# Attention with the order of each engine given in the source, scores and maxima in single PSUM banks, and q and k laid out turned

## The chip, the cores and the metric

The kernel runs on one core of a Trainium2 chip. Its engines are PE (matrix products; PEld is its weight load), DVE (vector), ACT (scalar functions), POOL (GpSimd) and SP, which here only issues DMA transfers. PE writes to PSUM, eight banks of 512 fp32 words in each of 128 partitions; DVE and ACT read PSUM, POOL does not. The metric is the device time of one launch in microseconds, as the median of several runs.

## The reference

Block-sparse attention over 4 batches of 8 heads, 768 positions and 64 features, followed by a feed-forward part:

```python
scores = scale * np.matmul(q, k.transpose(0, 1, 3, 2))
mask = np.abs(blk_i - blk_j) <= window                    # blocks of 32, window 1
mask = mask | (blk_i == 0) | (blk_j == 0) | (blk_i == n_blocks - 1) | (blk_j == n_blocks - 1)
...                                                       # and three sampled blocks per row of blocks
scores = np.where(mask, scores, -1000000000.0)
scores = scores - np.max(scores, axis=-1, keepdims=True)
attn = np.exp(scores)
attn = attn / (np.sum(attn, axis=-1, keepdims=True) + 1e-09)
x = np.matmul(attn, v)                                    # heads joined: 3072 tokens x 512
h = x @ w_in                                              # 512 x 2048
out = (h - np.tanh(h)) @ w_out                            # 2048 x 512
```

All of it is in fp32. The kernel reaches that precision by splitting each factor into a high and a low part and adding up products of the parts.

## The kernel before, in words

The 32 heads are worked on in 16 pairs. A pair's q and k come from DRAM with the positions in partitions (`load`). `prep_qk` (line 192) transposes each of them on PE in six steps (line 198), copies the result to an fp32r tile on ACT (the high part, line 200) and subtracts that from it on DVE (the low part, line 201). `dist` (line 204) then spreads the parts by twelve DMA transfers of 64 partitions over four operands, `sA` to `sD`, in one of three slots of SBUF, where the rows 64 to 87 hold the mask as 24 rows of blocks (`fill`) and row 88 of `sB` the negative row maximum. One matmul with 88 or 89 rows so adds the mask, and with row 88 the maximum, to a product of the high parts.

Per head there are six key tiles of 128 keys, each against all 768 queries. Each passes these steps:

- `smax` (line 248): the products of the high parts with 128 queries against all keys in 512 + 256 columns, in a PSUM tile of two banks, and a maximum over them on DVE (line 259). After six of these `smax_fin` (line 261) turns the maxima on PE, scales them on DVE (line 266) and sends them to row 88 of `sB` by a DMA that SP issues (line 267). These maxima run about ten tiles ahead of the scores.
- `qk_exp` (line 276): the scores, turned (keys in partitions), in 512 + 256 columns of two passes each (lines 283 and 284), in a PSUM tile of two banks, and one exponential of 768 columns on ACT to `pe` (line 287).
- `split` (line 290): `ph`, an fp16 copy of `pe` (on ACT, line 297, or for two tiles of twelve on DVE, line 295), and `pl`, the fp16 rest (line 299), on POOL, or for one tile of twelve on DVE.
- `accum` (line 303): 18 matmuls of 64 or 65 columns that add the tile's products of `ph` and `pl` with the parts of v. After six tiles `norm` (line 325) divides by the sum of the row, and `spill` writes the pair's result to DRAM.

`prep_v` (line 217) scales and splits v for each pair, with the low part on DVE (line 241). Six of the feed-forward part's weight tiles are loaded and converted from their 8-byte words during attention (`load_pre` and `convert_pre`); each conversion is three DVE instructions (`convert`, lines 436, 439 and 442).

PSUM holds three tiles of two banks (scores, maxima and the transposes share them) and two of one bank (the `accum` sums, the turned maxima, the sum for v).

The order of the work comes from a list of events, each with a time in units of one key tile (`at`, the constants in lines 55 to 62), sorted by time. The framework then places the instructions by a timeline of its own and may reorder them within an engine; three kinds of added dependences hold it back: a chain through the PE work from head 5 on (`in_order`), the first loads (`after`), and the value products in pairs (line 317). Whatever it chooses, each engine's sequence is fixed before the launch, and each engine runs its sequence in that order. Every DMA is issued by SP.

`FFN` is the feed-forward part. Its first two steps are placed at the end of attention, and the rest (`rest`, line 611) follows when attention's PSUM is free.

Of the kernel before, what the change touches and what calls it, by code (L numbers as in the profile page):

```python
# [106 lines left out]
def attention(ctx, tc, q, k, v, samp, w_in, w_out, blocks, xscr, ident, ps, slots, wt, f2, ffn):  # L107
    nc = tc.nc
    big, one = ps
# [6 lines left out]
    loads = {}


    chain = []

    def in_order(h, first, last):
        if h < CH0:
            return
        if chain:
            tc.add_manual_dep(
                first.ins, chain[-1].ins.name, mybir.DependencyInfo(mybir.DependencyClass.NoSync, mybir.DependencyReason.DATA), reason="order"
            )
        chain.append(last)  # L130


    urgent = [[], [], []]

    def after(n, d):
        for f in urgent[n]:
            tc.add_manual_dep(
                d.ins, f.ins.name, mybir.DependencyInfo(mybir.DependencyClass.NoSync, mybir.DependencyReason.DATA), reason="first pair"
            )

    def load(pr, which="kqv", first=None):
        r = loads.setdefault(pr, [])
        for nm, src in ((n, x) for n, x in (("k", k), ("q", q), ("v", v)) if n in which):
            t = p2.tile([P, S], F32, tag="raw" + nm, name=f"raw{nm}{pr}", bufs=2)
            d = nc.sync.dma_start(out=t, in_=src[pr])
            r.append(t)
            if pr <= 3 and first is not None:
                after(first, d)

    load(0, "kq")  # L150
# [534 lines left out]
```

## Time and profile before

| | us |
|---|---|
| median of three runs | 985.01 |
| lowest and highest of them | 983.36 and 985.48 |
| span of the profiled execution, first to last instruction | 983.2 |

The profile gives no time of the profiled execution other than its span; the median of the runs stands 1.8 us above it. Over the span PE is busy 94%, DVE 75%, ACT 64% and POOL 47% of the time, as an average over attention and the feed-forward part. In the rows below a group reads: line, engine, operation, output<-inputs, shapes, number of instructions | busy time in us, mean length of one in ns | idle time of the engine before them, and what ended it. A timeline row reads: start, length, engine, line, operation, number, and in brackets the engine's idle time before it. In the windows each engine has its busy time in us and, in brackets, its number of instructions; PEclk is the granted clock of PE, and the DMA share that of 16 DMA engines.

### The profile page before, as it was taken

Reading aid. Unit: us, or ns where it says so; the run is one execution under the profiler, and the core shown is the slowest. Engines: PE = TensorE matmul, PEld = TensorE weight load, DVE = VectorE, ACT = ScalarE, POOL = GpSimd, SP = SyncE. Lnnn points to the kernel's source line nnn. Section 1 sums busy time; section 2 is a strip of 40 time slices with the busy share of each in tenths; the row PEclk is TensorE's granted clock in tenths of the full one; section 3 lists DMA queues with packets and bytes.
Section 4 is the critical chain, followed back from the end, with each engine's and each line's share of the span. In section 5 each row is a group of like instructions: output and inputs, shape, how many; then the busy total and the mean of one; then the engine's idle time right before and its main releaser. Section 6 shows DMA issues by size and latency. Waiting matters only on the chain.

```text
span 983.2 us, 18548 instructions
## 1 busy us (share of the span) xinstructions
PE 922.6 (94%) x7264; PEld 771.1 (78%) x7264; DVE 733.4 (75%) x1119; ACT 629.7 (64%) x943; POOL 458.3 (47%) x308
## 2 busy tenths in 40 slices
PE   5788999999999999888999999999999999999997
PEld 3577788887888878767788888888888888888885
DVE  4589888887887878859999876765676666566664
ACT  1476888888888878656666665555555465555553
POOL 1365877777777777754445422222222222222221
PEclk9698999999999999898999999999999999999999
DMA  8796777676676667114451220210020000001001
GB/s 231 185 274 190 195 175 175 162 174 162 168 173 162 162 161 189 45 48 157 148 168 50 65 76 11 97 33 12 1 75 1 1 33 11 1 1 44 1 1 43
DMA packets 56263, 99.78 MB, mean 101 GB/s; under 512 B 6008, under 2 KB 26680, under 8 KB 56176
## 3 DMA queue, kind: packets, MB, share of 16 engines
q1 hardware_dynamic: 56176, 98.60, 37.0%
q8 instruction: 57, 0.93, 0.4%
q14 instruction: 30, 0.25, 0.1%
HBM read 44.64 MB, written 15.20 MB: 61 GB/s over the span
## 4 chain that ended last, share of the span: by engine, by line
PE 77%; ACT 6%; DMA 5%; DVE 5%; issue 3%; SPq 1%; POOL 1%; ACTq 0%; POOLq 0%; DVEq 0%
PE pf L537 25%; PE pf L569 8%; PE pf L570 8%; PE pf L571 8%; PE st L283 6%; PE st L284 5%; PE sm L255 5%; ACT pe L287 3%; PE av L313 2%; PE av L321 2%; PE av L322 2%; DMA slot<-lok 2%; DMA slot<-nm 2%; DVE mc L259 1%; PE pf L451 1%
## 5 line engine op out<-in xcount | busy, mean ns | idle before, releaser
L299 POOL TENSOR_TENSOR pl<-pe,ph 128x768 f16<-128x768 f32 x173 | 290.0, 1692 | 130.5 <-ACT ph L297 67.5
L560 POOL TENSOR_TENSOR gl<-t,gh 128x512 fp32r<-128x512 f32 x96 | 124.0, 1292 | 358.4 <-ACT gh L559 307.0
L259 DVE TENSOR_REDUCE mc<-sm 128x1 f32<-128x768 f32 x192 | 181.0, 951 | 53.1 <-PE sm L255 49.2
L287 ACT ACTIVATE pe<-st 128x768 f32<-128x768 f32 x192 | 154.1, 805 | 78.4 <-PE st L284 68.5
L283 PE MATMUL st<-slot 128*128 128x512 f32 (+1 forms) x384 | 146.4, 382 | 17.1 <-ACT pe L287 13.4
L552 DVE TENSOR_TENSOR t<-t,pf 128x512 f32<-128x512 f32 x94 | 64.5, 686 | 123.3 <-ACT t L546 123.2
L559 ACT ACTIVATE gh<-t 128x512 fp32r<-128x512 f32 x96 | 60.6, 632 | 120.2 <-DVE t L556 120.2
L297 ACT ACTIVATE ph<-pe 128x768 f16<-128x768 f32 x154 | 130.0, 844 | 4.7
L284 PE MATMUL st<-slot 89*128 89x512 f32 (+1 forms) x384 | 126.1, 349 | 1.0 <-DMA slot<-nm 1.0
L313 PE MATMUL av<-vhl,ph 128*128 128x65 f16 x1152 | 120.7, 195 | 0.0
L322 PE MATMUL av<-vhl,pl 128*128 128x65 f16 x1152 | 119.6, 194 | 0.9 <-POOL pl L299 0.9
L255 PE MATMUL sm<-slot 88*128 88x512 f32 (+1 forms) x384 | 111.1, 376 | 9.6 <-DMA slot<-hiq 7.0
L321 PE MATMUL av<-vhl,ph 128*128 128x64 f16 x1152 | 119.7, 196 | 0.0
L313 PEld LDWEIGHTS <-ph 128*128 128x128 f16 x1152 | 106.6, 97 | 13.6 <-issue 12.9
L322 PEld LDWEIGHTS <-pl 128*128 128x128 f16 x1152 | 107.9, 100 | 3.0 <-issue 1.5
L321 PEld LDWEIGHTS <-ph 128*128 128x128 f16 x1152 | 107.9, 98 | 0.7 <-issue 0.5
L544 ACT ACTIVATE u<-pf 128x512 f32<-128x512 f32 x94 | 56.2, 598 | 80.5 <-PE pf L537 80.2
L283 PEld LDWEIGHTS st<-slot 128*128 128x128 f32 x384 | 74.9, 195 | 35.1 <-ACT pe L287 18.5
L284 PEld LDWEIGHTS st<-slot 89*128 89x128 f32 x384 | 75.5, 197 | 11.2 <-DMA slot<-nm 2.2
L255 PEld LDWEIGHTS sm<-slot 88*128 88x128 f32 x384 | 62.6, 202 | 17.0 <-DMA slot<-mk 6.3
L570 PE MATMUL pf<-wx,gh 128*128 128x512 f32 x192 | 74.7, 389 | 0.0
L569 PE MATMUL pf<-wx,gh 128*128 128x512 f32 x192 | 74.7, 389 | 0.0
(123 smaller groups left out, 1962.8 us busy)
## 6 DMA issues: line engine op xcount, KB each, us to landing
slot<-hik SPq DMA_DIRECT2D x64, 192.0 KB
slot<-hiq SPq DMA_DIRECT2D x64, 192.0 KB
stage<-w_in SPq DMA_DIRECT2D x13, 512.0 KB
stage<-w_out SPq DMA_DIRECT2D x13, 512.0 KB
rawk<-k SPq DMA_DIRECT2D x16, 384.0 KB
rawq<-q SPq DMA_DIRECT2D x16, 384.0 KB
slot<-lok SPq DMA_DIRECT2D x32, 192.0 KB
slot<-loq SPq DMA_DIRECT2D x32, 192.0 KB
```

What stands on the lines that cost most here:

```text
L255: nc.tensor.matmul(pm[:, c], lhsT=sB[s][0:88, j, t * P : (t + 1) * P], rhs=sA[s][0:88, j, c], start=True, stop=True)
L259: maxed.append(nc.vector.tensor_reduce(out=mcs[h][:, t : t + 1], in_=pm[:, 0:S], op=ALU.max, axis=AX.X))
L283: ms.append(nc.tensor.matmul(st[:, c], lhsT=sC[s][:, j, kc], rhs=sD[s][:, j, c], start=True, stop=False))
L284: ms.append(nc.tensor.matmul(st[:, c], lhsT=sA[s][0:89, j, kc], rhs=sB[s][0:89, j, c], start=False, stop=True))
L287: nc.scalar.activation(out=pe, in_=st[:, 0:S], func=AF.Exp, scale=0.125)
L299: d = eng.tensor_tensor(out=pl, in0=pe, in1=ph, op=ALU.subtract)
L313: m = nc.tensor.matmul(o[:, t, :], lhsT=ph[:, c], rhs=vv[:, 0:65], start=(kt == 0 and t == 0), stop=False, skip_group_check=True)
L321: nc.tensor.matmul(o[:, t, 0:64], lhsT=ph[:, c], rhs=vv[:, 65:129], start=False, stop=False, skip_group_check=True)
L322: m = nc.tensor.matmul(o[:, t, :], lhsT=pl[:, c], rhs=vv[:, 0:65], start=False, stop=last, skip_group_check=True)
L537: nc.tensor.matmul(h, lhsT=w[:, cc], rhs=x[:, c, :], start=(k == 0), stop=(k == 3 * NCT - 1))
L569: nc.tensor.matmul(o, lhsT=gh[:, c], rhs=wo[0][ft], start=(ft == f0), stop=False)
L570: nc.tensor.matmul(o, lhsT=gh[:, c], rhs=wo[1][ft], start=False, stop=False)
```

## The change

- **Order.** In attention, and in the feed-forward steps placed within it, every call to an engine goes through a wrapper (`InOrder`) that tells the framework to keep the instruction at its place in the program order of its engine. The sorted list of events so is the order of each engine, SP's issues included; the three kinds of added dependences are gone. The steps are cut finer, so that the list can interleave them.
- **q and k.** They are stored in DRAM turned, with two heads' features in the 128 partitions and k and q side by side, as one array `kq`, loaded by one DMA per pair. The raw fp32 words are spread as the high parts. For the low parts DVE clears the low 12 bits (`mask_words`, two instructions of 768 words) and the rest is found by a subtraction (`low_words`, k's on DVE, q's on POOL). The PE transposes, the ACT copies and the subtractions from PSUM are gone. The number and size of the spreading DMAs is as before.
- **PSUM.** Six single banks are used in turn for scores, maxima and the small turned tiles, and two hold the `accum` sums of even and odd heads. Two key tiles (1536 columns) take three banks: 512, 256 + 256, and 512 columns. Each bank has an exponential of 512 columns on ACT and a maximum on DVE; the six tiles' two partial maxima are joined by one more small DVE instruction a head.
- **Casts.** `pe`, `ph` and `pl` are tiles for two key tiles (1536 columns). ACT copies in two halves; for one of six such tiles DVE copies it at once; `pl` is always one POOL instruction of 1536 columns.
- **Places.** The maxima run 8 units (key tiles) ahead of the scores at the start and 12 later. The turned maxima of a head go out 3.25 units ahead of its scores in the steady stage. The first pair's q and k and the first two heads' maxima are issued on ACT's DMA queue. The weight conversions are spread, with an instruction every two units, three of each 24. The feed-forward part's first staged weights are loaded near the end of attention.

```diff
-W0, DW = 40, 24.7
+W0, DW = 42.9, 24
-PB = 8
+PB = 4
+NPE = 3
-TQK, TV, TSM, LSP, LAV = -15.1, -5.6, -9.95, 2.1, 4.2
-PL_DVE = (11,)
-PL_DVE_END = (2, 5, 8, 11)
-PH_DVE = (4, 10)
+LEAD = 12
+LAV = 5.35
+PH_DVE = (3,)
+RAMP, NRAMP = 4, 24
+LATE = {2: (14, 10, 6), 3: (8, 4, 3), 4: (5, 3, 2), 5: (2, 1, 1), 6: (1, 0.5, 0.5)}
...
+            def call(*args, **kw):
+                r = f(*args, **kw)
+                self.tc.keep_in_program_order(r)
+                return r
...
-        big = actx.enter_context(tc.tile_pool(name="ps_big", bufs=3, space=PSUM))
-        one = actx.enter_context(tc.tile_pool(name="ps_one", bufs=2, space=PSUM))
+        psum = actx.enter_context(tc.tile_pool(name="psum", bufs=1, space=PSUM))
+        banks = [psum.tile([P, 512], F32, name=f"ps{i}") for i in range(8)]
+        turn = iter(range(10**6))
+        ps = lambda: banks[next(turn) % 6], banks[6:]
...
+    def load_x(pr):
+        raws[pr] = p2.tile([P, 2 * S], F32, tag="rawx", name=f"rawx{pr}", bufs=2)
+        if pr:
+            nc.sync.dma_start(out=raws[pr], in_=kq[pr])
+        else:
+            for x in range(2):
+                nc.scalar.dma_start(out=raws[pr][:, half(pr, x)], in_=kq[pr][:, half(pr, x)])
...
-        for t in range(T):
-            nc.tensor.transpose(pt[:, t * P : (t + 1) * P], raw[:, t * P : (t + 1) * P], ident)
-        ptv = pt[:, 0:S]
-        nc.scalar.activation(out=hi, in_=ptv, func=AF.Copy)
-        nc.vector.tensor_tensor(out=lo, in0=ptv, in1=hi.bitcast(F32), op=ALU.subtract)
...
+    def mask_words(pr, x):
+        if x == 0:
+            los[pr] = p2.tile([P, 2 * S], F32, tag="lo", name=f"lo{pr}", bufs=2)
+        c = half(pr, x)
+        nc.vector.tensor_scalar(
+            out=los[pr].bitcast(I32)[:, c], in0=raws[pr].bitcast(I32)[:, c], scalar1=-4096, scalar2=None, op0=ALU.bitwise_and
+        )
+
+    def low_words(pr, x, eng):
+        c = half(pr, x)
+        eng.tensor_tensor(out=los[pr][:, c], in0=raws[pr][:, c], in1=los[pr][:, c], op=ALU.subtract)
...
+    PIECES = (((0, 0, 512),), ((0, 512, S), (1, 0, 256)), ((1, 256, S),))
...
+    def smax(n, x):
...
+        b = sms[n, x] = bank()
+        for e, c, o in pieces(x):
+            t = 2 * m + e
+            nc.tensor.matmul(b[:, o], lhsT=sB[s][0:88, j, t * P : (t + 1) * P], rhs=sA[s][0:88, j, c], start=True, stop=True, skip_group_check=True)
+
+    def most(n, x):
...
+        if x == 1:
+            nc.vector.tensor_reduce(out=mcs[h][:, o : o + 2], in_=b.rearrange("p (e c) -> p e c", e=2), op=ALU.max, axis=AX.X)
+        else:
+            nc.vector.tensor_reduce(out=mcs[h][:, o : o + 1], in_=b, op=ALU.max, axis=AX.X)
...
+    def most_send(h):
...
+        (nc.sync if h > 1 else nc.scalar).dma_start(
...
+    def scores(n, x):
...
+        for e, c, o in pieces(x):
+            kc = slice((2 * m + e) * P, (2 * m + e + 1) * P)
+            nc.tensor.matmul(b[:, o], lhsT=sC[s][:, j, kc], rhs=sD[s][:, j, c], start=True, stop=False, skip_group_check=True)
+            nc.tensor.matmul(b[:, o], lhsT=sA[s][0:89, j, kc], rhs=sB[s][0:89, j, c], start=False, stop=True, skip_group_check=True)
+
+    def exps(n, x):
+        if x == 0:
+            pes[n] = p2.tile([P, 2 * S], F32, tag="pe", name=f"pe{n}", bufs=NPE)
+        nc.scalar.activation(out=pes[n][:, 512 * x : 512 * (x + 1)], in_=sts.pop((n, x)), func=AF.Exp, scale=0.125)
+
+    def high(n, e):
...
+        if n % 6 not in PH_DVE:
+            c = half(None, e)
+            nc.scalar.activation(out=phs[n][:, c], in_=pes[n][:, c], func=AF.Copy)
+        elif e:
+            nc.vector.tensor_copy(out=phs[n], in_=pes[n])
+
+    def low(n):
+        pls[n] = p2.tile([P, 2 * S], F16, tag="pl", name=f"pl{n}", bufs=PB)
+        nc.gpsimd.tensor_tensor(out=pls[n], in0=pes.pop(n), in1=phs[n], op=ALU.subtract)
...
+    def smt(n):
+        return 2 * n - LEAD + RAMP * max(0, 1 - n / NRAMP)
+
+    for h in range(2 * NPAIR):
+        t0 = smt(3 * h + 2)
+        late = 0 if h < 4 else 2
+        at(t0 + 1.6, most_join, h)
+        at(t0 + 2.5 + late, most_turn, h)
+        at(t0 + 2.75 + late, most_send, h)
+        at(6 * h + 10.3, norm, h)
+    for n in range(6 * NPAIR):
+        for x in range(3):
+            at(2 * n + 0.45 * x, scores, n, x)
+            at(smt(n) + 0.45 * x + 0.25, smax, n, x)
+            at(smt(n) + 0.45 * x + 0.6, most, n, x)
+            at(2 * n + 0.45 * x + 0.4, exps, n, x)
+        at(2 * n + 1, high, n, 0)
+        at(2 * n + 1.6, high, n, 1)
+        at(2 * n + 1.7, low, n)
+        at(2 * n + LAV, accum, n)
...
     for x in range(2 * NPRE):
         at(W0 + DW * x, load_pre, "io"[x % 2], x // 2)
-        at(W0 + DW * x + 4, convert_pre, "io"[x % 2], x // 2)
+        for k in range(3):
+            at(W0 + DW * x + 6 + 2 * k, convert_pre, "io"[x % 2], x // 2, k)
...
-        "q": pairs(inputs["q"], 0, 2, 3, 1, 4),
-        "k": pairs(inputs["k"], 0, 2, 3, 1, 4),
+        "kq": np.concatenate([pairs(inputs[n], 0, 1, 4, 3, 2) for n in "kq"], axis=2),
```

More of the change, by code (lines that the diff above doesn't have):

```diff
@@ L116, in attention, with load_v, load_masks, ones @@
     sA, sB, sC, sD = ([slots[i][:, x] for i in range(NSLOT)] for x in range(4))
[L118 to L150, printed above, removed]
+    raws, rvs, los, ams, sbs = {}, {}, {}, {}, {}
+    R = slice(64, 88)
+    st_sb = acst.tile([P, 2 * NB + S], F32, name="st_sb")
+    mk = p2.tile([P, S], F32, tag="pe", name="mk", bufs=NPE)
+    onehot = st_sb[:, 2 * NB : 2 * NB + S]
+    def load_x(pr):
[5 more added lines that the diff above has]
+                nc.scalar.dma_start(out=raws[pr][:, half(pr, x)], in_=kq[pr][:, half(pr, x)])
+    def load_v(pr):
+        rvs[pr] = p2.tile([P, S], F32, tag="rawv", name=f"rawv{pr}", bufs=2)
+        nc.sync.dma_start(out=rvs[pr], in_=v[pr])
+    sp_i = acst.tile([P, 6], I32, name="sp_i")
+    def load_masks():
+        nc.sync.dma_start(out=sp_i[R, :], in_=samp)
+        nc.sync.dma_start(out=st_sb[R, :], in_=blocks)
+    def ones(i):
+        nc.gpsimd.memset(sA[i].bitcast(F32)[64:89], 1.0)
     def setup():
@@ L217, in prep_v, with fill @@
[L217 to L232 removed]
+    def fill(i, dst, src):
+        nc.sync.dma_start(out=dst[i].bitcast(F32)[R], in_=src[R, :].unsqueeze(1).to_broadcast([NB, 2, S]))
@@ L234, in prep_v, with v_turn, v_scale @@
+    def v_turn(pr):
+        am, ams[pr] = ams[pr], bank()[:, 0:P]
+        nc.tensor.matmul(ams[pr], lhsT=am.to_broadcast([P, P]), rhs=ident, start=True, stop=True)
+    def v_scale(pr):
+        sb = sbs[pr] = p2.tile([P, 1], F32, tag="sb", name=f"sb{pr}", bufs=4)
+        nc.vector.tensor_reduce(out=sb, in_=ams.pop(pr), op=ALU.max, axis=AX.X)
         sbi = sb.bitcast(I32)
@@ L249, in smax @@
+    mcs, sms = {}, {}
+    def smax(n, x):
+        h, m = divmod(n, T // 2)
         pr, j = divmod(h, 2)
         s = pr % NSLOT
[L251 to L259 removed]
@@ L303, in accum @@
[L303 to L323 removed]
+        b = sts[n, x] = bank()
@@ L354, in attention @@
-    at(TQK + 0.3, fill, 0, sA, mask, 0)
-    at(TQK + 0.9, load, 1, "kq", 0)
-    at(TQK + 1.7, load, 0, "v", 1)
-    for i in range(1, NSLOT):
-        for dst, src in ((sB, onehot), (sA, mask)):
-            at(TQK + TF * i, fill, i, dst, src, 1)
+    at(-50, load_masks)
+    for i in range(NSLOT):
+        at(-48, ones, i)
+    at(-47, setup)
+    at(-46, fill, 0, sB, onehot)
+    at(-26.5, fill, 0, sA, mk)
+    for i, t in ((1, -4.5), (2, 6)):
+        at(t, fill, i, sB, onehot)
+        at(t + 0.5, fill, i, sA, mk)
@@ new lines, in attention @@
+        when = (s - 29.2, s - 25.2, s - 23.2) if pr > 1 else (-1, 0.7, 2.8) if pr else (-28, -28, -28)
+        at(when[0], mask_words, pr, 0)
+        at(when[1], mask_words, pr, 1)
+        at(when[2], low_words, pr, 0, nc.vector)
+        at(when[2], low_words, pr, 1, nc.gpsimd)
+        for x, (j, what) in enumerate(ORDER):
+            at(t0 + late[2] - 21 + x if pr > 1 else x - 3 if pr else EARLY[x], dist, pr, j, what)
+        s = t0 + (10.5, 4)[pr] if pr < 2 else t0
+        at(s - 9.3, v_most, pr)
```

308 lines of the change are left out of this document (119 added, 189 removed).

## The prediction

> **What bounds the kernel now.** First the windows of all engines, cut at the first exponential, where the pace settles, at the last exponential, and where the feed-forward part is at pace; then the same windows for the exponentials alone (L287).
>
> ```profile
> span 983.2 us, 18548 instructions
> ...
> core 0: us, PE busy (x) PEld busy (x) DVE busy (x) ACT busy (x) POOL busy (x), PEclk, DMA share, GB/s
> 33.40:105.20 71.80, 63.56 (x704) 52.89 (x703) 60.54 (x89) 49.57 (x62) 47.39 (x27) 0.88 0.80 226
> 105.20:428.30 323.10, 304.47 (x4060) 262.60 (x4059) 264.14 (x402) 265.29 (x339) 245.51 (x150) 0.99 0.62 155
> 428.30:446.00 17.70, 9.65 (x97) 7.69 (x96) 9.85 (x18) 5.99 (x11) 4.81 (x3) 0.82 0.35 111
> 446.00:983.20 537.20, 529.79 (x2360) 436.64 (x2360) 383.24 (x584) 304.34 (x529) 155.93 (x121) 0.99 0.14 45
> ...
> 33.40:105.20 71.80, 24.16 (x30) 0.88 0.80 226
> 105.20:428.30 323.10, 129.91 (x162) 0.99 0.62 155
> ```
>
> The last 537 us are the feed-forward part, with PE full; the change leaves them alone. Attention has two stages. Steady: 162 key tiles in 323.1 us, 1.994 each, 23.9 us per pair of heads (12 tiles), over 13.5 pairs. Start: the first exponential at 33.4, then 30 tiles in 71.8 us where the steady pace needs 59.8. In the steady stage DVE and ACT are busy 82% and POOL 76%; PE's 94% is partly the modelled ends. So next, PE's starts (start, length, line):
>
> ```profile
> 252.15 0.82 PE L198 MATMUL ptk<-ident,rawk 128*128 128x128 f32 x6
> 252.80 0.27 PE L264 MATMUL pmt<-ident,mc 128*6 128x128 f32 x1
> ...
> 259.24 0.20 PE L313 MATMUL av<-vhl,ph 128*128 128x65 f16 x1
> ...
> 260.35 0.48 PE L283 MATMUL st<-slot 128*128 128x512 f32 x1
> ...
> 261.16 0.51 PE L255 MATMUL sm<-slot 88*128 88x512 f32 x2
> 261.50 0.40 PE L283 MATMUL st<-slot 128*128 128x512 f32 x1
> ```
>
> Two tiles' value products take 260.35 - 259.24 = 1.11 us, one tile's scores and maxima products 261.50 - 260.35 = 1.15. Two tiles: 3.41; a pair of heads 20.5, and 1.3 more for twelve transposes (0.65 per six): 21.8 of 23.9. PE leads, but nothing is full; the rest is lost in turns between engines.
>
> **The change, part by part, for one pair of heads.** The prices, by groups of instructions (the L299 and L295 rows of DVE are of the steady stage alone), then three single instructions:
>
> ```profile
> L259 DVE TENSOR_REDUCE mc<-sm 128x1 f32<-128x768 f32 x192 | 181.0, 951 | 53.1 <-PE sm L255 49.2 <-PE av L322 1.8
> L552 DVE TENSOR_TENSOR t<-t,pf 128x512 f32<-128x512 f32 x94 | 64.5, 686 | 123.3 <-ACT t L546 123.2
> L299 DVE TENSOR_TENSOR pl<-pe,ph 128x768 f16<-128x768 f32 x16 | 24.8, 1551 | 2.6 <-ACT ph L297 1.7
> L295 DVE CAST ph<-pe 128x768 f16<-128x768 f32 x32 | 22.2, 693 | 6.0 <-ACT pe L287 6.0
> L201 DVE TENSOR_TENSOR lok<-ptk,hik 128x768 fp32r<-128x768 f32 x16 | 15.2, 947 | 0.0
> L287 ACT ACTIVATE pe<-st 128x768 f32<-128x768 f32 x192 | 154.1, 805 | 78.4 <-PE st L284 68.5 <-POOL pl L299 8.1 <-POOL slot L498 0.7
> L546 ACT ACTIVATE t<-pf 128x512 f32<-128x512 f32 x94 | 55.8, 593 | 0.2 <-POOL gl L560 0.2
> L200 ACT ACTIVATE hik<-ptk 128x768 fp32r<-128x768 f32 x16 | 12.8, 797 | 18.7 <-DVE mc L259 13.1 <-PE ptk L198 5.6
> L560 POOL TENSOR_TENSOR gl<-t,gh 128x512 fp32r<-128x512 f32 x96 | 124.0, 1292 | 358.4 <-ACT gh L559 307.0 <-issue 29.8 <-PE pf L537 21.0
> ...
> 109.79 3.25 POOL L299 TENSOR_TENSOR pl<-pe,ph 128x768 f16<-128x768 f32 x2
> 46.01 0.55 DVE L295 CAST ph<-pe 128x768 f16<-128x768 f32 x1
> 63.97 0.94 DVE L299 TENSOR_TENSOR pl<-pe,ph 128x768 f16<-128x768 f32 x1
> ```
>
> *PE.* The transposes go: -1.3. Scores and maxima keep their columns and their count of matmuls (512 + 256 + 256 + 512 over two tiles instead of twice 512 + 256). PE: 20.5.
>
> *ACT.* Three 512-wide exponentials for two tiles instead of two 768-wide: 3 x 0.593 - 2 x 0.805 = +0.17, +1.0 per pair; the two copies L200 go, -1.6. Casts stay 768 wide. Net -0.6 from 265.3/13.5 = 19.7. ACT is no bound.
>
> *DVE.* Maxima 3 x 0.686 (the nearest 512-wide row that reads PSUM) - 2 x 0.951 = +0.16, +0.9 per pair; two small joins, no row, between nothing and 0.3 each, taken at 0.3 together. L201 goes, -1.9; in come two mask operations of 768 words (nearest row the 0.55 cast, upper end 0.95) and one subtraction from SBUF (0.94). The DVE share of `pl` goes (-0.94); two casts of 0.55 become one of twice the width (0.55 to 1.1, taken 0.95). The weight conversions, now all in the start, are spread out, 18 instructions over the 16 pairs: 18 x 0.6 / 16 = +0.65 (nearest row L552). Today's 264.1/13.5 = 19.6 holds 0.9 of waiting (1.55 for a 0.94 subtraction, 2 x 0.14 in the casts), so 18.7 becomes about 19.6 without waits.
>
> *POOL.* All `pl` now run here, as six instructions of 1536 elements, and q's subtraction of 768 fp32 words (1.65 as the 768 row, or 768/512 x 1.292 = 1.94; taken 1.75). Two 768s in a row take 3.25, the upper end. A line through 512 (1.29) and 768 (1.65) gives 1.4 ns an element and 2.73, the lower end; but those two rows differ in type, and the 768 row is the same form, so I stay near doubling: 3.1. The Trainium skill, GPSIMD Engine Reference, section 3.1, gives 4497 ns for 2048 elements of two fp32 inputs; in proportion 1536 would be an estimated 3.37, and with that page's price the sum below would be 25.1 and the time about 988.
>
> POOL and DVE also take turns. Start, length, line:
>
> ```profile
> 99.79 6.79 POOL L299 TENSOR_TENSOR pl<-pe,ph 128x768 f16<-128x768 f32 x4
> 102.22 1.26 DVE L295 CAST ph<-pe 128x768 f16<-128x768 f32 x1 [0.52 <-ACT pe L287]
> 65.25 5.59 POOL L299 TENSOR_TENSOR pl<-pe,ph 128x768 f16<-128x768 f32 x3 [5.02 <-ACT ph L297]
> 65.70 2.02 DVE L241 SCALAR_TENSOR_TENSOR vhl<-rawv,sb,vhl 128x768 f16<-128x768 f32 x1
> 423.62 5.91 POOL L299 TENSOR_TENSOR pl<-pe,ph 128x768 f16<-128x768 f32 x3 [1.37 <-DVE ph L295]
> 425.79 2.23 DVE L299 TENSOR_TENSOR pl<-pe,ph 128x768 f16<-128x768 f32 x1
> 58.14 2.09 POOL L299 TENSOR_TENSOR pl<-pe,ph 128x768 f16<-128x768 f32 x1 [1.44 <-DVE sb L235]
> ```
>
> A DVE instruction that casts SBUF to SBUF or reads two SBUF tiles stretches to the end of the POOL instruction under way (the 0.94 subtraction takes 2.23), and POOL's next one then stretches: four in 6.79 instead of 6.45 (a cast costs POOL 0.34), three in 5.59 instead of 4.85 (0.74), one in 2.09 instead of 1.65 (0.44, in the weight conversions). After the change a pair of heads has two masks (2 x 0.34), a subtraction (0.74), a double cast (0.6), the v split (0.74) and conversions (18 x at most 0.44 / 16, taken 0.4): 3.15 us taken from POOL. POOL's period: 6 x 3.1 + 1.75 + 3.15 = **23.5**; with 2.73 and 1.65 it is 21.2, with 3.25 and 1.94 24.6. It passes PE's 20.5 and becomes the longest. The gain on PE and ACT is therefore hidden: against 23.9 the steady stage gives 0.4 x 13.5 = **-6** (bounds -36 and +9).
>
> *Order.* Every engine had one fixed order before as well; what alters is which. The row maxima of a head go out 3.25 tiles ahead of its scores (6.5 us) instead of 4.9 (9.8 us). Behind that transfer PE's scores are queued, and ACT and POOL behind them:
>
> ```profile
> 111.26 2.01 DMA slot<-nm
> ...
> 314.09 4.88 DMA slot<-nm
> ```
>
> Landing takes 2.0 to 4.9, so some 1.5 us of cover stay: 0. Without cover each microsecond costs 1 per head, 27 in all. SP issues the same twelve spreading transfers per pair, and the wider bank and buffer turns (six single banks, three double `pe`, four double `ph` and `pl`) hold as many tiles as before or more: 0.
>
> *Start.* The path to the first exponential:
>
> ```profile
> 5.44 1.54 PE L198 MATMUL ptk<-ident,rawk 128*128 128x128 f32 x6 [5.44 <-POOL ident masks.py:199]
> 14.20 6.50 PE L255 MATMUL sm<-slot 88*128 88x512 f32 x16 [5.94 <-DMA slot<-hiq]
> 22.14 0.27 DVE L266 TENSOR_SCALAR nm<-pmt 6x128 fp32r<-6x128 f32 x1
> 25.10 7.05 DMA slot<-nm
> 33.46 0.82 ACT pe L287
> ```
>
> k and q are spread as they land, no later than 5.44, without transposes and copies; then the mask's fill is last, and the first maxima begin at about 11.5 instead of 14.2. Nine reductions of 0.61 (0.686 less the 0.08 by which neighbours overlap), join, turn and scale end near 18.5 instead of 22.4. The transfer leaves at once on ACT's queue (SP issues it at 25.10, 2.7 late) and lands in 2 to 5 instead of 7.05. That is 22 to 25 for 33.46: **-10**. The stage loads and the early weight loads also leave these 105 us, where the DMA share is 0.80 against 0.62 later; of the 12 us lost there I take back **-3** (0 to -12). The end of attention keeps its 17.7 us: 0 (POOL loses DVE's help with the last `pl`, up to +5).
>
> Sum: 983.2 - 6 - 10 - 3 = 964; the median stands 1.8 above this span: **966**.
>
> **Rivals.** *POOL is not the bound* (wide instructions save a fixed cost): at 2.73 POOL needs 21.2, near PE's 20.5; steady -36, start -13: 936. For it: the two widths; against: their types.
>
> *DVE is held up at the port.* Each of about six DVE instructions a pair that share the port with POOL now finds 3.1 us instructions instead of 1.65. A mean wait of half of one, 1.55, when POOL is busy gives a period X = 18.7 + 9.5 x 20.3/X, so 26.1: +2.2 x 13.5 = +30, with the start's -13 about 1002. (18.7 instead of 19.6, since neighbouring instructions overlap.) It decides once the mean wait passes (23.5 - 18.7)/6.1 = 0.8 us. For it: 2.02 and 2.23 above; against: today's steady casts and v splits wait little, since they fall when POOL waits for them. The Trainium skill, SBUF - State Buffer, section Who interferes with whom, has the pair of ports held exclusively for a whole instruction; the rows above agree, and it speaks against long POOL instructions.
>
> *It changes next to nothing*: POOL at the upper end, 24.6, takes back +9 of the start's -13, which gives 981; or queue heads (SP's above all) lose all that the start gives, 985. For it: the same form in a row, 3.25; against: nothing but the unlike widths.
>
> **How the numbers follow.** Forecast (955 to 978) 0.40; POOL free (930 to 955) 0.22; next to nothing (978 to 990) 0.14; DVE held up (above 990) 0.24. Time 966; 936 to 1002 leaves about 0.2 outside; the forecast's own range is 955 to 978. Within 0.2% (2 us, about what a measurement can tell) is 0.05; faster 0.40 + 0.22 + 0.05 = 0.67; slower 0.28.
>
> **What would show it.** A `pl` row near 3.1 and POOL over 90% busy in the steady stage; first exponential before 26; mask and subtraction rows on DVE far above 0.55 and 0.94 (the port); PE waiting for `pl`. A `pl` near 2.7 makes the forecast too slow; DVE over 95% busy, with PE waiting for the maxima, too fast; scores waiting for `nm` break the order's zero.

## The result, and the profile after

The changed kernel takes **1005.75 us** (median of four runs, 1005.28 to 1009.0), the kernel before on the same chip 984.18: a ratio of 1.0231 (95% interval 1.0210 to 1.0251). It is slower, and lies beyond the upper end of the range, 1002; the forecast was 966.

From here on all rows of attention's instructions carry L79, the line of the wrapper, so the tiles tell them apart. First lines of the changed kernel's page, then the chain in that of the kernel before:

```profile
span 1004.0 us, 18122 instructions
...
PE 62%; DVE 24%; DMA 7%; issue 4%; ACT 2%; SPq 0%; POOL 0%; DVEq 0%; ACTq 0%; POOLq 0%
```

```profile
PE 77%; ACT 6%; DMA 5%; DVE 5%; issue 3%; SPq 1%; POOL 1%; ACTq 0%; POOLq 0%; DVEq 0%
```

DVE has 24% of the chain that ended last; before, it had 5%. The windows have the same bounds as those of the kernel before:

```profile
core 0: us, PE busy (x) PEld busy (x) DVE busy (x) ACT busy (x) POOL busy (x), PEclk, DMA share, GB/s
33.40:105.20 71.80, 58.55 (x694) 48.73 (x693) 61.58 (x100) 46.61 (x71) 54.14 (x19) 0.88 0.60 148
105.20:428.30 323.10, 286.38 (x3675) 235.58 (x3673) 306.42 (x476) 245.74 (x367) 274.31 (x88) 0.94 0.66 166
```

In the steady stage DVE was busy 264.1 us of 323.1 and is now busy 306.4 (95%); POOL went from 245.5 to 274.3 (85%); PE fell from 304.5 to 286.4, at a granted clock of 0.94 instead of 0.99. The span splits up at three exponentials (the first of all, the first of head 5, the end of the last):

| | before | after | difference |
|---|---|---|---|
| to the first exponential | 33.5 | 26.3 | -7.2 |
| heads 0 to 4 | 72.0 | 75.1 | +3.1 |
| from head 5 to the last exponential's end | 322.6 | 343.6 | +21.0 |
| from there to the end | 555.1 | 559.0 | +3.9 |

The sum is the 20.8 us between the spans. The measure for the rest of this text is the **steady period**, per pair of heads: the time from the exponential that opens head 5 to the one that opens head 27, over eleven pairs. It was (368.5 - 105.5)/11 = 23.91 and is (385.1 - 101.4)/11 = 25.79 us. The loss lies in these eleven pairs (20.7 us): the last five heads, from the second of the two exponentials to the end of the last one, take 59.9 us and took 59.6. The changed kernel's groups, and after them a view by tile whose three numbers are the shortest, the median and the longest in ns:

```profile
L79 DVE TENSOR_SCALAR lo<-rawx 128x768 int32<-128x768 int32 x32 | 55.7, 1742 | 2.2 <-DMA rawv<-v 2.2
L79 DVE SCALAR_TENSOR_TENSOR vhl<-rawv,sb,vhl 128x768 f16<-128x768 f32 x16 | 32.9, 2055 | 0.5 <-ACT vhl L79 0.5
L79 DVE TENSOR_TENSOR lo<-rawx,lo 128x768 f32<-128x768 f32 x16 | 30.2, 1886 | 0.0
L79 DVE CAST ph<-pe 128x1536 f16<-128x1536 f32 x16 | 20.0, 1253 | 2.3 <-ACT pe L79 2.3
```

```profile
L79 DVE TENSOR_SCALAR lo<-rawx x32: 546/1980/3078, 7.1 to 371.8; 128x768 int32<-128x768 int32 x32
L79 DVE TENSOR_TENSOR lo<-rawx,lo x16: 952/1877/2628, 8.0 to 375.7; 128x768 f32<-128x768 f32 x16
...
L79 DVE SCALAR_TENSOR_TENSOR vhl<-rawv,sb,vhl x16: 1004/2104/2450, 37.5 to 418.6; 128x768 f16<-128x768 f32 x16
...
L79 DVE CAST ph<-pe x16: 944/946/2712, 46.6 to 439.5; 128x1536 f16<-128x1536 f32 x16
...
L79 POOL TENSOR_TENSOR pl<-pe,ph x96: 3085/3126/3838, 30.5 to 449.5; 128x1536 f16<-128x1536 f32 x96
L79 POOL TENSOR_TENSOR lo<-rawx,lo x16: 1845/2532/2552, 8.3 to 376.7; 128x768 f32<-128x768 f32 x16
```

The shortest are the instructions undisturbed. What lies above them is waiting: for the masks 55.7 - 32 x 0.546 = 38.2 us, for k's subtraction 15.0, for v's low part 16.8, for the casts 4.9. Together 74.9 us, 0.94 for each of the 80 instructions. The eighteen instructions of the weight conversions go from SBUF to SBUF too, and by the same working wait 10.8 us more. Of the sum, 71.2 us fall to instructions that start in the steady stage: 5.7 per pair (323.1/25.79 = 12.5 pairs). DVE's busy 306.4 us are 24.5 per pair; without the waits it is 18.8. POOL's side of the same stage:

```profile
L79 POOL TENSOR_TENSOR pl<-pe,ph 128x1536 f16<-128x1536 f32 x77 | 253.0, 3302 | 48.8 <-DVE ph L79 25.4 <-ACT ph L79 11.9 <-issue 4.6
L79 POOL TENSOR_TENSOR lo<-rawx,lo 128x768 f32<-128x768 f32 x11 | 27.4, 2488 | 0.0
```

Above the 3.126 (the median) and 1.845 that they take undisturbed, POOL's instructions lose 77 x 0.176 + 11 x 0.643 = 20.6 us, 1.6 per pair. Two stretches of the timeline show how they arise, DVE first, then POOL:

```profile
207.98 1.48 DVE L79 TENSOR_SCALAR lo<-rawx 128x768 int32<-128x768 int32 x1
209.38 1.28 DVE L79 TENSOR_REDUCE mc<-ps 128x2 f32<-128x512 f32 x2
210.58 0.94 DVE L79 CAST ph<-pe 128x1536 f16<-128x1536 f32 x1
...
213.44 2.11 DVE L79 SCALAR_TENSOR_TENSOR vhl<-rawv,sb,vhl 128x768 f16<-128x768 f32 x1
...
216.96 1.98 DVE L79 TENSOR_SCALAR lo<-rawx 128x768 int32<-128x768 int32 x1
...
220.85 1.87 DVE L79 TENSOR_TENSOR lo<-rawx,lo 128x768 f32<-128x768 f32 x1
...
205.90 3.14 POOL L79 TENSOR_TENSOR pl<-pe,ph 128x1536 f16<-128x1536 f32 x1 [0.39 <-POOL pl L79]
211.60 10.30 POOL L79 TENSOR_TENSOR pl<-pe,ph 128x1536 f16<-128x1536 f32 x3 [2.56 <-DVE ph L79]
```

The mask of 207.98 ends at 209.46, shortly after the POOL instruction of 205.90 (209.04); undisturbed it needs 0.55. Behind it on DVE stand two maxima and the cast that POOL itself waits for: POOL idles 2.56 us until it has come. Then POOL runs three instructions, 3.43 us each on average, which end at 214.74, 218.52 and 221.90. The next three DVE instructions of these kinds keep step with them: they end at 215.55, 218.94 and 222.72. The waits of the steady stage (who waited for whom: total, times, longest):

```profile
PE ps L79 <- DVE mc L79: 29.2, 38, 2.2
...
POOL pl L79 <- DVE ph L79: 24.3, 11, 2.6
...
PE ps L79 <- DMA slot<-nm: 5.8, 3, 4.4
...
DVE mc L79 <- PE ps L79: 2.7, 9, 0.6
```

Before, in the same stretch (105 to 400 us):

```profile
DVE mc L259 <- PE sm L255: 37.0, 47, 2.6
```

Then DVE waited 37.0 us for PE's maxima products; now it waits 2.7, and PE waits 29.2 for DVE to read its banks.

### The profile page after: what moved, and what is told of

The parts are those of the page before. It is cut to its first block, busy times and chain, and to the rows that moved or that the text cites. A ratio compares the mean times of both kernels' runs of the same rounds, so it can differ in the third digit from the quotient of the medians.

```text
span 1004.0 us, 18122 instructions
## 1 busy us (share of the span) xinstructions
PE 914.0 (91%) x7072; PEld 752.5 (75%) x7072; DVE 786.9 (78%) x1222; ACT 625.9 (62%) x1013; POOL 519.4 (52%) x247
## 4 chain that ended last, share of the span: by engine, by line
PE 62%; DVE 24%; DMA 7%; issue 4%; ACT 2%; SPq 0%; POOL 0%; DVEq 0%; ACTq 0%; POOLq 0%
PE pf L561 25%; PE ps L79 12%; DVE mc L79 9%; PE pf L593 8%; PE pf L594 8%; PE pf L595 8%; DVE lo L79 5%; DVE vhl L79 2%; DMA slot<-nm 2%; DMA slot<-lo 2%; DVE ph L79 1%; DMA xscr<-xq 1%; DVE xq L79 1%; PE pf L475 1%; DVE cvto L79 1%
## 5 line engine op out<-in xcount | busy, mean ns | idle before, releaser
L79 POOL TENSOR_TENSOR pl<-pe,ph 128x1536 f16<-128x1536 f32 x96 | 313.6, 3281 | 87.0 <-ACT ph L79 41.8
L79 PE MATMUL ps<-slot 89*128 89x512 f32 (+5 forms) x1152 | 271.1, 376 | 55.5 <-DVE mc L79 31.1
L79 PEld LDWEIGHTS ps<-slot 89*128 89x128 f32 (+2 forms) x1152 | 189.8, 205 | 89.8 <-DVE mc L79 44.6
L79 ACT ACTIVATE pe<-ps 128x512 f32<-128x512 f32 x288 | 169.1, 592 | 102.4 <-PE ps L79 94.2
L79 DVE TENSOR_REDUCE mc<-ps 128x1 f32<-128x512 f32 (+1 forms) x288 | 186.6, 679 | 25.8 <-PE ps L79 25.5
L79 PEld LDWEIGHTS <-ph 128*128 128x128 f16 x2304 | 117.7, 101 | 27.5 <-issue 27.2
L79 ACT ACTIVATE ph<-pe 128x768 f16<-128x768 f32 x160 | 135.0, 844 | 5.0
L79 PE MATMUL ps<-vhl,ph 128*128 128x65 f16 (+1 forms) x2304 | 129.7, 200 | 3.2 <-DVE vhl L79 2.3
L79 PE MATMUL ps<-vhl,pl 128*128 128x65 f16 x1152 | 124.4, 198 | 6.2 <-POOL pl L79 6.2
L79 PEld LDWEIGHTS <-pl 128*128 128x128 f16 x1152 | 111.8, 103 | 9.0 <-POOL pl L79 9.0
L580 DVE COPY_PREDICATED t<-mk,pf 128x512 f32<-128x512 int32 x94 | 69.7, 742 | 6.9 <-DVE pf L579 0.5
L561 PE MATMUL pf<-slot,wx 128*128 128x512 f32 x288 | 70.3, 391 | 0.4 <-DVE t L580 0.4
```

The costliest lines, as they stand in the source:

```text
L79: r = f(*args, **kw)
L561: nc.tensor.matmul(h, lhsT=w[:, cc], rhs=x[:, c, :], start=(k == 0), stop=(k == 3 * NCT - 1))
L580: nc.vector.copy_predicated(t, mk.bitcast(I32), h)
```

## The experiments

The theories: (1) DVE and POOL hold each other up at their shared port, since the low parts of q and k no longer read PSUM and POOL's instruction is twice as long; (2) the fixed order costs; (3) the wide POOL instruction or POOL's share of work costs by itself. The measured values of all runs, each with the kernel before on the same chip:

| kernel | us | ratio to before (95%) | steady period |
|---|---|---|---|
| changed kernel | 1005.75 | 1.0231 (1.0210 to 1.0251) | 25.79 |
| e1, low parts moved together | 1007.01 | 1.0218 (1.0188 to 1.0247) | 26.23 |
| e2, order left free | 1018.8 | 1.0346 (1.0290 to 1.0401) | 26.85 |
| e3, `pl` in halves | 985.9 | 1.0026 (1.0001 to 1.0050) | 24.84 |
| e4, no low parts of q, k | 959.6 | 0.9744 (0.9706 to 0.9782) | 21.75 |
| e5, casts on ACT | 988.0 | 1.0054 (1.0034 to 1.0073) | 24.24 |
| e6, low parts by way of PSUM | 984.5 | 1.0028 (1.0001 to 1.0055) | 23.83 |
| e7, e6 with `pl` in halves | 988.4 | 1.0057 (1.0033 to 1.0081) | 24.18 |
| e8, e6 with casts on ACT | 978.0 | 0.9946 (0.9923 to 0.9969) | 23.01 |
| e9, e1 with casts on ACT | 1047.4 | 1.0665 (1.0627 to 1.0703) | 29.37 |
| e10, e8 with DVE's help at the end | 974.4 | 0.9923 (0.9897 to 0.9948) | 23.25 |
| e11, e10 with maxima sent earlier | 968.5 | 0.9873 (0.9826 to 0.9920) | 22.75 |
| e12, e6 with POOL's work kept | 986.3 | 1.0026 (0.9996 to 1.0057) | 24.24 |

**e4: the low parts of q and k left out** (zeros are spread in their place, so the scores lack those products' low parts; all transfers stay).

```diff
-        at(when[0], mask_words, pr, 0)
-        at(when[1], mask_words, pr, 1)
-        at(when[2], low_words, pr, 0, nc.vector)
-        at(when[2], low_words, pr, 1, nc.gpsimd)
+        los[pr] = zlo
```

> The changed kernel with the low parts of q and k left out: the masks and both subtractions are not done, and zeros are spread in place of the low parts by the same transfers. Prices that part. Theory 1 (DVE and its waits are the bound): 6.2 us less on DVE per pair of heads (2 x 2.1 + 1.9) and 2.5 less on POOL; PE's 20.5 and POOL's 20.4 are next, so a period of 21.5 to 22.5 and 950 to 962. Theory 3 (POOL is the bound): 2.5 less, about 972. Theory 2: above 990.

As expected. The three DVE instructions of a pair and POOL's one (2.45 us, which goes with them) are worth 4.0 us of period; undisturbed, DVE's are 2 x 0.546 + 0.952 = 2.0. Without them the changed kernel is 2.6% faster than the kernel before: the loss sits in these instructions and what they set off.

**e2: the order left free** for the framework's placing.

```diff
-                self.tc.keep_in_program_order(r)
```

> The changed kernel without the hold on program order: the framework's planner may place the instructions on each engine as it did in the kernel before; everything else stays. Theory 2 (the fixed order is what costs): below 990. Theory 1 (the port): DVE's port instructions still meet POOL instructions of 3.1 us, so 995 to 1010, with mask rows still well above 0.55. Theory 3: the same as theory 1.

13 us slower than the changed kernel, in two runs that lie 7 us apart, and beyond what theory 1 allowed: the period is 1.06 longer, and the first exponential comes at 41.7 instead of 26.3. With this list the fixed order is a gain; theory 2 falls. Theory 1's expectation of the masks fails here too:

```profile
L79 DVE TENSOR_SCALAR lo<-rawx 128x768 int32<-128x768 int32 x32 | 19.8, 656 | 37.3 <-DMA rawx<-kq 33.6 <-DMA slot<-rawx 3.7
```

The masks hardly wait (656 ns), since the framework often puts them where DVE has stood still for the load of q and k (33.6 us over the run). The waits of the 80 instructions come to 36 us, half of the changed kernel's, and the period is longer all the same, so other waits set it; this run neither supports theory 1 nor tests it.

**e3: `pl` as two POOL instructions of 768.** Nothing of DVE's work changes, and POOL's grows.

```diff
-        nc.gpsimd.tensor_tensor(out=pls[n], in0=pes.pop(n), in1=phs[n], op=ALU.subtract)
+        pe = pes.pop(n)
+        for e in range(2):
+            c = half(None, e)
+            nc.gpsimd.tensor_tensor(out=pls[n][:, c], in0=pe[:, c], in1=phs[n][:, c], op=ALU.subtract)
```

> The changed kernel with the POOL subtraction for pl as two instructions of 768 columns instead of one of 1536; nothing else. Theory 1 (the port): the longest wait falls from 3.1 to 1.6 and the sum of waits per pair of heads from 6 to about 3; then POOL's own sum, 6 x 3.2 + 2.0 + 3.15 = 24.4, is next, so 1005 - 1.5 x 13.5 = 985. Theory 3 (POOL's work is the bound): POOL's work grows by 0.1 to 0.15 per instruction, so 1005 to 1015. Theory 2: 1005.

Groups of this run:

```profile
L79 POOL TENSOR_TENSOR pl<-pe,ph 128x768 f16<-128x768 f32 x192 | 347.4, 1841 | 46.0 <-ACT ph L79 21.6 <-DVE ph L79 17.1 <-issue 5.0
L79 DVE TENSOR_SCALAR lo<-rawx 128x768 int32<-128x768 int32 x32 | 38.7, 1212 | 3.1 <-DMA slot<-lo 3.1
L79 DVE SCALAR_TENSOR_TENSOR vhl<-rawv,sb,vhl 128x768 f16<-128x768 f32 x16 | 32.4, 2024 | 0.6 <-ACT vhl L79 0.6
```

20 us faster although POOL is busier (347.4 us for `pl` instead of 313.6): POOL's work by itself is not what costs, and that part of theory 3 falls. The masks fell from 1742 to 1212 ns; v's low part did not. POOL has 12 x 1.84 + 2.0 = 24.1 us of work in a period of 24.84, and DVE is as full (280.1 and 282.3 us of the 295 from 105 to 400). The halves also let POOL start on the first half while the second is cast; POOL waits 11.3 us for DVE's cast in that stretch, where it waited 24.3. This run alone does not part the two gains; e7 bears on it.

**e6: the masked words written to a PSUM bank**, and the subtraction reading them there, for k and q on DVE in three pieces of 512; POOL does none of it.

```diff
+        c = slice(512 * x, 512 * (x + 1))
+        b = bank()
...
-            out=los[pr].bitcast(I32)[:, c], in0=raws[pr].bitcast(I32)[:, c], scalar1=-4096, scalar2=None, op0=ALU.bitwise_and
+            out=b.bitcast(I32), in0=raws[pr].bitcast(I32)[:, c], scalar1=-4096, scalar2=None, op0=ALU.bitwise_and
         )
...
-        eng.tensor_tensor(out=los[pr][:, c], in0=raws[pr][:, c], in1=los[pr][:, c], op=ALU.subtract)
+        nc.vector.tensor_tensor(out=los[pr][:, c], in0=raws[pr][:, c], in1=b, op=ALU.subtract)
```

> The changed kernel with q and k's masked words written to a PSUM bank, 512 columns at a time, and the low part found by DVE as SBUF minus PSUM, so that neither instruction should need the port shared with POOL (in the kernel before such forms did not stretch); all six instructions on DVE, none on POOL. DVE's work without waits grows by 1.6 us per pair of heads (6 x 0.6 instead of 2 x 0.55 + 0.94), POOL's falls by 2.5. Theory 1 (the port): the 4.1 us of waits at these instructions go; period 23.3 to 23.6, time about 973. If DVE's own work were the bound, without the port: 1005 + 1.6 x 13.5 = 1027. Program order in itself: 1005.

**e12: the same, with POOL keeping 768 words of subtraction per pair**, because e6 also took work from POOL. (q's low part is zero here and left out of the scores.)

```diff
+    def q_low(pr):
+        c = half(pr, 1)
+        nc.gpsimd.tensor_tensor(out=los[pr][:, c], in0=raws[pr][:, c], in1=raws[pr][:, c], op=ALU.subtract)
```

> As e6_low_from_psum, where DVE writes the mask words to a PSUM bank and subtracts from there, but POOL keeps one subtraction of 768 fp32 words per pair, as in the changed kernel (of q's raw words from themselves, so that q's low part is zero and left out of the scores; everything that depends on it runs as before). e6 took two things from the changed kernel at once: DVE's waits at the port, and 2.45 us of POOL's work per pair. This run gives the second back. If the waits were what cost (theory: DVE and POOL at the port), the mask and subtraction rows on DVE stay at 0.68 us and the period stays near e6's 23.8, at most 24.4, because POOL with 80% busy has room; 984 to 992 us. If POOL's own work was what e6 saved, the period goes back to near the changed kernel's 25.8; 1000 us or more.

Groups of e6, then of e12:

```profile
L79 DVE TENSOR_TENSOR lo<-rawx,ps 128x512 f32<-128x512 f32 x48 | 33.0, 687 | 3.0 <-issue 1.4
L79 DVE TENSOR_SCALAR ps<-rawx 128x512 int32<-128x512 int32 x48 | 32.8, 683 | 0.0
L79 DVE SCALAR_TENSOR_TENSOR vhl<-rawv,sb,vhl 128x768 f16<-128x768 f32 x16 | 31.5, 1971 | 0.5 <-ACT vhl L79 0.5
```

```profile
L79 DVE TENSOR_SCALAR ps<-rawx 128x512 int32<-128x512 int32 x48 | 32.7, 684 | 0.2 <-DMA rawx<-kq 0.2
L79 POOL TENSOR_TENSOR lo<-rawx 128x768 f32<-128x768 f32 x16 | 24.3, 1516 | 0.5 <-DMA rawx<-kq 0.5
```

In e6 DVE's own work for the low parts doubles, from 2.0 to 3 x (0.683 + 0.687) = 4.1 us per pair, and yet the period falls by 1.96: all 96 instructions take 0.68, POOL busy or not. v's low part, which writes SBUF as before, still takes 1971. e6 missed its 973: the period is 0.2 to 0.5 longer than expected, and where the rest of the 11 us lies is not shown. e12 gives POOL a subtraction back and keeps most of the gain (25.79 to 24.24), as theory 1 says. It isn't an exact price of POOL's work: the subtraction takes 1.52 here where it took 2.45, and DVE, without q's, does 3.2 us per pair instead of 4.1.

**e1: DVE's instructions that share the port placed directly ahead of the cast**, where POOL waits for DVE anyway (masks, k's subtraction and v's low part in a run, once a pair).

```diff
+        c = t0 - (28.6 if pr > 3 else 16.6)
+        when = (c, c + 0.05, c + 0.1) if pr > 2 else (s - 29.2, s - 25.2, s - 23.2) if pr > 1 else (-1, 0.7, 2.8) if pr else (-28, -28, -28)
...
-        at(t0 + (8.45, 4, 0)[min(pr, 2)] - 4.45, v_parts, pr, 0)
+        at(t0 + (8.45, 4, -2)[min(pr, 2)] - 4.45, v_parts, pr, 0)
```

> The changed kernel with the same instructions and only DVE's places moved: from the fourth pair on the two masks, k's subtraction and the low part of v stand right ahead of the one cast in six that DVE makes, for which POOL waits anyway. Theory 1 (the port): in the changed kernel the DVE instructions that share the port with POOL wait some 6 us per pair of heads in all, behind POOL instructions of 3.1 us, and DVE sets the period of 25.9; here one wait opens the port for all four, so the period falls to POOL's 23.7 (6 x 3.1 + 2.0 + 3.15) and the time by 2.2 x 12 = 26, to about 980. Theory 2 (program order in itself, queue heads on PE and SP) and theory 3 (POOL is the bound): within 4 of 1005.

A clear miss. A stretch of DVE's timeline, and the waits of the steady stage, in this run:

```profile
213.12 2.74 DVE L79 TENSOR_SCALAR lo<-rawx 128x768 int32<-128x768 int32 x2
215.78 0.94 DVE L79 TENSOR_TENSOR lo<-rawx,lo 128x768 f32<-128x768 f32 x1
216.65 0.68 DVE L79 TENSOR_REDUCE mc<-ps 128x1 f32<-128x512 f32 x1
217.25 1.00 DVE L79 SCALAR_TENSOR_TENSOR vhl<-rawv,sb,vhl 128x768 f16<-128x768 f32 x1
218.18 0.95 DVE L79 CAST ph<-pe 128x1536 f16<-128x1536 f32 x1
```

```profile
POOL pl L79 <- DVE ph L79: 46.5, 11, 4.2
PE ps L79 <- DVE mc L79: 33.1, 25, 3.3
```

The subtraction, v's part and the cast run undisturbed now, and over the run the masks take 1320, k's subtraction 1211, v's part 1288 and the cast 981 ns: by the same working as above 34 us of waits instead of 74.9. The weight conversions, which stay where they were, wait 22.7 us instead of 10.8. With them the sum falls from 85.7 to 57 us, and nothing came of it. In the 6 us from 213.12 to 219.13 DVE reads one maximum; POOL waits up to 4.2 us for the cast at the end of the run, and PE up to 3.3 for a bank. So the sum of DVE's waits is not the whole price. As these rows have it, it also counts what is queued behind them, and how long DVE stays away from PE's banks at one time.

**e5: all casts on ACT**, so that POOL waits for no DVE instruction: `PH_DVE = ()` instead of `(3,)`.

> The changed kernel with the one fp16 cast in six that DVE makes moved to ACT (all casts on ACT, in two halves); nothing else. Prices the place where POOL waits for DVE: in the changed kernel POOL stands 2.1 us per pair of heads before that cast, and DVE gives it 1.2. Refined theory 1 (DVE and POOL lock each other out, so each wait on one side becomes one on the other): 25.9 - 1.2 to 25.9 - 2.1, so 978 to 990; ACT gets 1.5 more, to about 21 of 24, and is no bound. If the cast costs nothing: 1005.

18 us faster, within what was expected; POOL's waits for DVE's cast (24.3 us in the steady stage) are gone, and the masks wait as before (1788). Of the 1.55 us of period up to 0.94 is the cast's own time, for which ACT has room. That the rest came of POOL's waits for DVE is not shown: POOL now waits 24.4 us for ACT's casts in the steady stage (6.9 in the changed kernel), and v's part also fell, from 2055 to 1762 ns.

**e9: e1 and e5 together.**

> DVE's port instructions together (as in the first run) and all casts on ACT (as in the fifth). In the first run the waits of DVE at the port fell from 6 to about 2.5 us per pair of heads and the time did not; POOL then stood 4 us per pair before DVE's cast, which was queued behind the others. If that is why, the gain must appear once no cast is queued there: period near 22.7, time about 970, clearly below the fifth run's 988. If the five microseconds of DVE work in a row are themselves the harm (PE waits for the maxima behind them): 988 or more.

The largest miss, on the side of the second expectation. DVE's and POOL's timelines around one such run, and the steady stage's waits:

```profile
200.56 6.40 DVE L79 TENSOR_SCALAR lo<-rawx 128x768 int32<-128x768 int32 x2
...
193.91 12.64 POOL L79 TENSOR_TENSOR pl<-pe,ph 128x1536 f16<-128x1536 f32 x4
```

```profile
PE ps L79 <- DVE mc L79: 63.0, 19, 9.1
```

And all the masks of the run, by tile:

```profile
L79 DVE TENSOR_SCALAR lo<-rawx x32: 545/2288/6107, 7.6 to 408.1; 128x768 int32<-128x768 int32 x32
```

In e1 POOL stood still during the run, since it waited for the cast at its end. With the cast on ACT, POOL goes on without a gap until 206.55: the first mask waits for one POOL instruction and the second for the next, 6.40 us for 1.1 of work. The longest mask of the run (316.78 to 322.89) waits for two POOL instructions in a row, which end at 319.42 and 322.47. PE waits up to 9.1 us for a bank in this run. The rows show it so; with how many banks PE would ride through such a run was not tried.

**e7: e6 and e3 together.**

> The run before this one (low parts by way of PSUM) and pl as two POOL instructions of 768. Theory 1: what is left of DVE's waits (the v split, the cast, the conversions; 2 us per pair of heads) falls to about 1.2; POOL 12 x 1.75 = 21; period 22.7 to 23, about 964. If the waits no longer matter by then, the same as the run before.

A miss. With the masks away from the port, halving `pl` gains nothing: v's part still takes 2021 ns, as in e3, and `pl` costs POOL 327.3 us instead of 308.2. So what the halves gained in e3 was most likely the masks' waits, and not the earlier start of POOL, which e7 has too. Nor does the wide instruction cost anything by itself here, so the other part of theory 3 falls. Why v's part isn't shortened by shorter POOL instructions stays open.

**e8: e6 and e5 together.**

> Low parts by way of PSUM and all casts on ACT, pl in one instruction of 1536. Theory 1: DVE at 21.4 - 0.95 and some 1.8 of waits, POOL 6 x 3.2 = 19.2 and no longer waiting for DVE's cast; PE's 20.5 and ACT's 21 are near; period 22 to 22.5, about 957.

Faster than the kernel before, by 0.5% (0.3 to 0.8), though far from 957. In its steady stage PE waits 9.0 us, in five times, for the row maxima `nm`, and v's part still takes 2199.

**e10: e8, with DVE's help at the end of attention**: of the 96 tiles for two keys, every second cast from number 86 on is DVE's, and half of each `pl` from number 92 on.

```diff
+            for e, eng in enumerate((nc.gpsimd, nc.vector)):
+                c = half(None, e)
+                eng.tensor_tensor(out=pls[n][:, c], in0=pe[:, c], in1=phs[n][:, c], op=ALU.subtract)
```

> The version of the eighth run (low parts by way of PSUM, casts on ACT) with DVE's help at the end, where the maxima are over, DVE is busy a third of the time and ACT 97%: from the 87th of 96 tile pairs DVE makes every second cast, from the 93rd the second half of pl. The last five ACT casts of 1.5 and three halves of 1.55 leave the chain: 3 to 6 us, 972 to 975. If the end is set by PE or by the first feed-forward step: 978.

**e11: and the turned maxima one unit earlier**: `late = 0 if h < 4 else 1` instead of 2.

> The run before this one with the row maxima turned and sent one unit (about 2 us) earlier from the third pair on. In the eighth run's steady stage PE waits 9 to 11 us for their landing in 275 us, five times: that should go, 3 to 9 us less than the run before, about 967. If PE then waits for the joins of the maxima instead: no gain.

Both medians lie near what was expected. For e10 the trace doesn't bear the reason out: its interval overlaps e8's, the stretch from the last exponential to the end is 558.0 us where e8 has 558.8, and the last `pl` ends 6.5 us after that exponential, in e8 5.2. Windows of e11:

```profile
33.40:105.20 71.80, 59.06 (x704) 47.74 (x703) 59.78 (x114) 51.51 (x79) 46.61 (x16) 0.90 0.65 155
105.20:400.00 294.80, 274.25 (x3781) 225.41 (x3780) 279.54 (x503) 259.95 (x399) 249.28 (x79) 1.00 0.69 187
```

PE has a granted clock of 1.00. Its waits for the landing of `nm` in the steady stage, 12.1 us in e10, are gone, and those for DVE's maxima rose from 7.4 to 14.3. DVE is busy 95% of that stretch again, now with a period of 22.75. At 968.5 us e11 is faster than the kernel before by 1.3% (0.8 to 1.7) and than the changed kernel by some 36 us: the change's order, banks and layout, with the low parts of q and k away from the port and the casts, but for the end, on ACT.

## Why the prediction was wrong

**The step that failed** is POOL's sum as the longest of the steady stage, beside DVE at "about 19.6 without waits". The prediction put the turns of the two engines at the port down as a loss of POOL's alone, 3.15 us per pair, and DVE's waits at nothing, which it left to a rival. The runs show the reverse: DVE waits 5.7 us per pair and POOL loses 1.6. So DVE, with 24.5 us, became the fullest engine, and POOL, with 21.9, was busy 85% and not over 90%.

| per pair of heads, us | prediction | measured |
|---|---|---|
| `pl`, 1536 elements | 3.1 | 3.085 to 3.13 undisturbed |
| taken from POOL at the port | 3.15 | 1.6 |
| DVE without waits | 19.6; 18.7 with overlaps taken off | 18.8 |
| DVE's waits at the port: forecast, rival | 0, 9.5 x 20.3/26.1 = 7.4 | 5.7 |
| mean of one such wait: deciding, rival's while POOL is busy | 0.8, 1.55 | 0.94 |
| steady period: forecast, rival | 23.5, 26.1 | 25.79 |

The rival *DVE is held up at the port* had the place and the mechanism right. That its time, 1002, comes so near to 1005.75 is partly luck: its steady stage, +30, was +21.0, and its start, -13, was -4.1, with +3.9 at the end. (In the third rival the sum of 985 leaves out the steady -6; with it the time is 979.)

The argument that kept its chance at 0.24 was the error: "today's steady casts and v splits wait little, since they fall when POOL waits for them". That held for the casts and splits of before (medians 0.550 and 1.009). The change put three more at the port that stand anywhere, and they wait 53 of the 74.9 us; v's part itself went to 2055 ns on average.

That the port is the main cause is shown by three results together: 2.0 us of DVE's work, with POOL's 2.45, are worth 4.0 of period (e4), shorter POOL instructions gain in spite of more work (e3), and so does the way round by PSUM with twice DVE's work, or one and a half times (e6, e12). That the loss stops where these instructions do fits it: the last mask starts at 371.8, and from 385.1 on attention takes as long as before. What the rival lacked is that a held DVE instruction also holds what is queued behind it and keeps DVE from PE's banks: e1 and e9 show such stretches, and e1 and e2 halve the waits of the 80 instructions without a gain. How the price splits up between these was not measured. The Trainium skill, SBUF - State Buffer, section Who interferes with whom, states an exclusive lock for a whole instruction; the rows of 200.56 and 216.96 agree.

**PE and ACT.** That their gain would be hidden was right. PE, 20.5 by the prediction, is no bound at 25.79; how near it lies is seen in e4, 21.75 with PE at 93%.

**POOL.** The `pl` instruction came as worked out; q's subtraction took 1.85 undisturbed and 2.45 on average, where 1.75 was taken. In proportion to a figure of the Trainium skill, GPSIMD Engine Reference, section 3.1, the estimate for `pl` was 3.37. The trace has 3.085 to 3.13, so the measurement decides: for this form, with one fp16 input and fp16 out, the estimate is 8% high. The rival with 2.73 falls.

**Order.** The zero for the new order against the old one was not measured. e2 shows only that the new list, left to the framework, is 13 us slower, with the first exponential 15.4 us later. The cover of the row maxima did not quite hold: PE waits 5.8 us for `nm`, three times, in the steady stage (before, 0.2). Where DVE is relieved it counts: e11 is 6 us faster than e10, with intervals that just overlap and a period 0.50 shorter.

**Start.** -10 became -7.2. Timeline of the changed kernel:

```profile
17.74 0.27 DVE L79 TENSOR_SCALAR nm<-ps 6x128 fp32r<-6x128 f32 x1
...
18.43 1.59 ACTq L79 DMA_DIRECT2D slot<-nm  x1
...
25.44 5.06 PE L79 MATMUL ps<-slot 89*128 89x512 f32 x15 [6.08 <-DMA slot<-nm]
...
26.27 0.60 ACT L79 ACTIVATE pe<-ps 128x512 f32<-128x512 f32 x1 [4.93 <-PE ps L79]
```

The scale came at 17.74 and ended at 18.0, a little before the forecast 18.5, and the issue followed at once. But the landing took 25.44 - 18.43 = 7.0, as before (7.05), not 2 to 5: the term mis-sized is the transfer. The further -3 for the next heads became +3.1; DVE was busy 61.6 of 71.8 us there, but what set it was not tried.

**End.** 0, "up to +5", became +3.9. The timeline's last rows of POOL and ACT:

```profile
443.33 9.23 POOL L79 TENSOR_TENSOR pl<-pe,ph 128x1536 f16<-128x1536 f32 x3
...
444.39 0.58 ACT L79 ACTIVATE pe<-ps 128x512 f32<-128x512 f32 x1
```

POOL ends 452.56 - 444.97 = 7.6 us after the last exponential; before it was 432.33 - 428.07 = 4.3, with DVE's help. That the missing help is the cause is not shown: e10 has it again, and its last `pl` still ends 6.5 us after the last exponential.

## What to carry to other kernels

Before an operation is moved from a form that reads PSUM to one within SBUF, count the DVE instructions that would run beside POOL's, and price each at up to one whole POOL instruction (here and there it was two in a row, 6.1 us in e9); a wider POOL instruction raises that price for all of them. A PSUM bank for the intermediate took DVE's masks and subtractions off the port here, at twice the work and still with a gain. Ask then what stands behind the held instruction on DVE, and above all whether POOL waits for it, and how long PE's banks last while DVE is away.

## What the runs showed of the hardware

- Writing integer words to a PSUM bank and subtracting from there took DVE 0.683 and 0.687 us for 512 words in all 96 instructions of e6, with POOL busy beside them; from SBUF to SBUF the mask of 768 took from 0.546 to 3.078.
- In e9 two such masks in a row took 6.40 us beside POOL instructions without a gap, each until one of these ended: DVE did not keep the port between them. One mask alone waited for two POOL instructions (6.107 us).
- POOL's time per element falls by only 6% with twice the width: 3.09 us for 1536 elements, against 1.65 for 768 in the kernel before. With two fp32 inputs and an fp32 output 768 take 1.85 undisturbed, and 1.52 where both inputs are the same tile (e12).
- The granted clock of PE in the steady stage was 0.99 before and 0.94 after; from 105 to 400 us it was 1.00 in e11 and 0.88 in e9. It is lowest in e9, where PE waits 63.0 us for DVE to read its banks, but does not follow PE's busy share alone: 0.97 in e3 with PE busy 89% of these 295 us, 0.94 in e7 with 91%. The prediction had no term for it.
